# Two transformer layers on one core: the residual kept as two chunks in SBUF, larger rings, and a different order for the last 256 queries

## The chip, the core and the metric

The kernel runs on one core of a Trainium2 chip. The metric is the device time of one execution in microseconds (us). A core has five engines, each with its own in-order list of instructions: TensorE (PE in the profile, with its weight loads as PEld), VectorE (DVE), ScalarE (ACT), GpSimd (POOL), and SyncE (SP), which here issues all DMAs. The engines meet only through semaphores. SBUF is the on-chip memory of 128 partitions, PSUM holds the matrix products in eight banks of 128x512 float32 values, and HBM is the memory outside.

## The reference

Two identical layers with the same weights are applied to `x` of 2048 tokens by 512 features, in bfloat16. Each layer is a pre-norm attention with 32 heads of 16 features and a pre-norm feed-forward network (FFN) of 1792 hidden features:

```python
x = x + _A_ref(_layernorm(x), A_wqkv, A_wo)
x = x + _B_ref(_layernorm(x), B_w1, B_b1, B_w2, B_b2)
x = x + _A_ref(_layernorm(x), A_wqkv, A_wo)
x = x + _B_ref(_layernorm(x), B_w1, B_b1, B_w2, B_b2)

def _A_ref(x, wqkv, wo):
    qkv = (x @ wqkv) reshaped to q, k, v of 32 heads of 16
    p = softmax(q k^T * 16 ** -0.5)
    return (p v, heads put side by side) @ wo

def _B_ref(x, w1, b1, w2, b2):
    return gelu(x @ w1 + b1) @ w2 + b2
```

## The kernel before, in words

**Tiling.** The 2048 tokens are 16 tiles of 128 (`NT`), in four chunks of 512 queries. The residual `X` lies in SBUF whole, 16 tiles of 512 bfloat16 values per partition. Attention works in passes (`passes`, L1034). A pass takes one chunk of queries and four heads, one in each quarter of the PE rows, and goes over the key tiles. One key tile of one head for 512 queries is a *cell*: one score matmul into one PSUM bank (L1168), an exponential, and one matmul of the weights with the values, called PV (L1566). There are 4096 cells, 512 for each layer and chunk. The last chunk of the second layer is cut into two segments of 256 queries (L1044), whose cells hold two heads of 256 queries. The scores of later chunks run while the FFN of the chunk before is done in the gaps.

**Two ways to an exponential.** Most cells go to ACT, two or three at a time from one slot of PSUM banks (`exps`, L1503), into a ring of `PT_RING` = 19 units of SBUF. Units that lie in other tensors are lent to this ring for a time (`lend_units`; the profile names them kt, q and v). Cells of four key tiles of each layer (`KD`, L45) may go to DVE instead, which is 1024 of the 4096. There a cell is one instruction that turns the scores into the bits of an approximate exponential (`dfirst`, L1317), and then two that make three shifted copies of it (`dchain`, L1378 and L1380). PV takes four matmuls for such a cell, three of them with scaled copies of V (`vc`). These cells live in the buffers `DU`. `DU` = 9 means four buffers for two cells each and one for a single cell, which the profile calls dh. In the second layer there is one more for two cells, in the freed K of the first layer (kt in the profile). A cell of `KD` that finds no buffer, bank or time on DVE before its pass has run out goes to ACT as the others do (`next_act`, `next_d`, `attach`, `swap`).

**What sets the order.** The order of all instructions is written when the program is built. `_Sched.run` (L353) plays the five engines with a cost for every operation. It takes for each engine the operations whose operands are ready by that reckoning, the one with the lowest priority number first, and appends it to that engine's list with the semaphore waits that it needs. On the chip the lists are fixed. An operation that comes late there holds up all that stands behind it on its engine. Scores have priority 0. Matmuls of projections and FFN have `FPRIO` = 1.5 for the first half of a product and `MID` = 1.4 for the second, and PV has 2, or 0.5 when a ring is nearly empty. `fill` (L331) adds matmuls without use (L1156) where PE would be idle too long.

**After a segment's attention.** `norm` divides by the softmax sums and writes `OTN`. `post` (L971) then spawns `wo` (the product with Wo, added to `X` at L816), the layernorm `ln`, `hpair` (the first FFN product, seven pairs), `gelu`, and `ytile` (the second FFN product, added to `X` at L956). In the first layer follow a layernorm and the projections to K, V and Q of the second. `before(l, seg)` (L967) names the segment ahead, and three waits of the plan go by it: `ofree` in `norm`, and `xfree` and `gfree` in `post`. They keep `OTN`, `XF` and `G` from being overwritten while the segment ahead still reads them. For the second segment of 256 queries, the one ahead is the first segment of the same chunk.

**Transfers.** `loads` (L572) brings in `X` and the weights of the first projections at the start, chunks 1 to 3 of `X` with one DMA each. `wloads` (L826) brings in all later weights in pieces of 256 KB through a ring of four (`W_RING`), each when a place in the ring is free. Layernorm transposes of 128 tokens are DMAs on SP too (L637).

Of the kernel before, what the change touches and what calls it, by code (L numbers as in the profile page):

```python
# [5 lines left out]
ALU = mybir.AluOpType  # L6
ACT = mybir.ActivationFunctionType
BF16 = mybir.dt.bfloat16
# [4 lines left out]
D = 512  # L13
# [5 lines left out]
NL = 2  # L19
# [3 lines left out]
DBANK = (7,)  # L23
PT_RING = 19
LEND = (3, 2)
QP_RING = 3
W_RING = 4
W_MORE = 4
XLN_RING = 2
GP = 2  # L30

DU = 9
LNP = 7
# [18 lines left out]
EVAC = 0.4  # L52
MID = 1.4
QUEUE = 4
RUSH = 4
# [372 lines left out]
def bass_interleave_layers__mha_block__dense_activation_gelu__prompt_kernel(  # L428
# [15 lines left out]
    with ExitStack() as es:  # L444
        def sb(shape, dt, name):
            return es.enter_context(nc.sbuf_tensor(name, shape, dt))

        T = {}
        T["X"] = sb([128, NT, D], BF16, "x")
        wr = sb([128, W_RING, 1024], BF16, "wr")  # L450
# [20 lines left out]
        if DU % 2:  # L471
# [23 lines left out]
        sem_names = ["pe", "act", "dve", "pool", "dxt0", "dxt1", "dxt2", "dxt3", "dx1", "dx2", "dx3", "dwq", "dwk", "dwv", "db1", "db2"] + ["dw%d" % c for c in range(3)] + [  # L495
                     "dout"] + ["dwr%d" % i for i in range(W_RING + W_MORE)] + ["dtr%d" % i for i in range(XLN_RING)]
        sems = {n: es.enter_context(nc.semaphore("s_" + n)) for n in sem_names}
        P = _Prog(sems)
        hbm = dict(x=A_x.rearrange("b (n p) d -> p (b n) d", p=128), out=out.rearrange("b (n p) d -> p (b n) d", p=128),
                   wqkv=A_wqkv, wo=A_wo, w1=B_w1, b1=B_b1, w2=B_w2, b2=B_b2)  # L500
# [32 lines left out]
class _Plan:  # L533
# [38 lines left out]
    def loads(self):  # L572
        T, hbm = self.T, self.hbm

        def load(dst, src, sem, keys, cost):
            return _Op("sp", cost, lambda e: e.dma_start(dst, src), writes=keys, sem=sem, by=16, tail=2.0)

        def lx(c):
            return load(T["X"][:, 4 * c:4 * c + 4, :], hbm["x"][:, 4 * c:4 * c + 4, :], "dx%d" % c,
                        ["X.%d" % t for t in range(4 * c, 4 * c + 4)], 2.5)  # L580
# [22 lines left out]
        yield ("give", "loaded")  # L603

    def ln(self, tiles, dst, dkeys, prio, quick=False):

# [3 lines left out]
        for t in tiles:  # L610
            yield ("need", ("xready", t, self.phase[t // 4]))
            yield _Op("dve", 0.66, lambda e, t=t: e.bn_stats(T["STATS"][:, t, :], T["X"][:, t, :]),
                      reads=["X.%d" % t], writes=["ST.%d" % t])
            yield _Op("dve", 0.17, lambda e, t=t: e.bn_aggr(T["MV"][:, t, :], T["STATS"][:, t, :]),
                      reads=["ST.%d" % t], writes=["MV.%d" % t])
# [12 lines left out]
    def ln_tile(self, c, t, dst, dkeys, quick):  # L628
# [4 lines left out]
        yield _Op(eng, cost, lambda e: e.tensor_scalar(  # L633
            T["XLN"][:, x, :], T["X"][:, t, :], T["RSTD"][:, t:t + 1], T["NMR"][:, t:t + 1], op0=ALU.mult, op1=ALU.add),
            reads=["X.%d" % t, "RSTD.%d" % c, "NMR.%d" % c], writes=["XLN.%d" % x])
        if not quick:
# [161 lines left out]
    def wo(self, l, seg, t):  # L798
        T = self.T
        for gb in range(4):  # L800
            yield ("need", ("otn", l, seg, gb))
        us = []
        for j in range(2):
            us.append((yield ("need", ("w", l, seg, "O", j))))
        b = yield ("acq", "misc")
        pb = self.bank(b)
        q = slice((t % 4) * 128, (t % 4) * 128 + 128)
        fns = []
        for j in range(4):
# [6 lines left out]
        yield _Op("dve", DV, lambda e: e.tensor_tensor(out=T["X"][:, t, :], in0=T["X"][:, t, :], in1=pb, op=ALU.add),  # L816
                  reads=["B.%d" % b, "X.%d" % t], writes=["X.%d" % t])
        yield ("rel", "misc", b)
        yield ("give", ("xready", t, 2 * l + 1))
# [55 lines left out]
    def hpair(self, l, seg, p):  # L875
# [8 lines left out]
        for j in range(2):  # L884
# [7 lines left out]
            for h in range(0, 4, FQ):  # L892
                yield _Op("pe", FQ * MM * n / 512, fns[4 * h:4 * h + 4 * FQ],
                          reads=["WR.%d" % w] + ["XF.%d" % (t % 4) for t in self.tiles(seg)],
                          writes=["B.%d" % b], prio=MID if h else FPRIO, mode="P")
            yield from self.wdone((l, seg, "1", p), w)
# [31 lines left out]
    def ytile(self, l, seg, t):  # L928
# [9 lines left out]
        for p in range(NFC // 2):  # L938
# [15 lines left out]
            if not tail or p == last:  # L954
                yield from self.wdone(piece, w)
        yield _Op("dve", DV, lambda e: e.tensor_tensor(out=T["X"][:, t, :], in0=T["X"][:, t, :], in1=pb, op=ALU.add),  # L956
                  reads=["B.%d" % b, "X.%d" % t], writes=["X.%d" % t])
        yield ("rel", "misc", b)
        yield ("give", ("xready", t, 2 * l + 2))
        if l == NL - 1:  # L960
            yield _Op("sp", 1.0, lambda e: e.dma_start(self.hbm["out"][:, t, :], T["X"][:, t, :]), reads=["X.%d" % t],
                      writes=["OUT.%d" % t], sem="dout", by=16, tail=2.0)

    def when(self, l, seg, part):
# [57 lines left out]
    def first(self, c):  # L1022
        T = self.T
        self.phase[c] = 0
        for t in range(4 * c, 4 * c + 4):
            yield ("give", ("xready", t, 0))
        tiles = range(4 * c, 4 * c + 4)
# [633 lines left out]
```

## Time and profile before

| | |
|---|---|
| time, median of 3 runs (lowest to highest) | 1567.77 us (1567.01 to 1567.84) |
| the profiled execution's own time | 1563.99 us |
| its span, first to last instruction | 1562.1 us |
| mean granted TensorE clock | 0.992 |
| ACT busy | 1523.5 us, 98% of the span |
| PE matmuls busy | 1443.7 us, 92% |
| DVE busy | 1369.9 us, 88% |
| POOL busy | 210.5 us, 13% |
| DMA traffic, share of 16 engines | 94.14 MB, 20.8% |

Busy times come from one profiled execution; they can be set against its own time, and the median of the runs lies 3.8 us above that. A line of the profile names the source line (L1503), the engine, the operation, the tile written and the tiles read, the shapes, and how often. A wait is put down to the instruction whose semaphore came last.

### The profile page before, as it was taken

Reading aid. Unit: us, or ns where it says so; the run is one execution under the profiler, and the core shown is the slowest. Engines: PE = TensorE matmul, PEld = TensorE weight load, DVE = VectorE, ACT = ScalarE, POOL = GpSimd, SP = SyncE. Lnnn points to the kernel's source line nnn. Section 1 sums busy time; section 2 is a strip of 40 time slices with the busy share of each in tenths; the row PEclk is TensorE's granted clock in tenths of the full one; section 3 lists DMA queues with packets and bytes.
Section 4 is the critical chain, followed back from the end, with each engine's and each line's share of the span. In section 5 each row is a group of like instructions: output and inputs, shape, how many; then the busy total and the mean of one; then the engine's idle time right before and its main releaser. Section 6 shows DMA issues by size and latency. Waiting matters only on the chain.

```text
span 1562.1 us, 42238 instructions
## 1 busy us (share of the span) xinstructions
PE 1443.7 (92%) x18537; PEld 432.7 (28%) x18537; DVE 1369.9 (88%) x2653; ACT 1523.5 (98%) x1412; POOL 210.5 (13%) x250
## 2 busy tenths in 40 slices
PE   8999889999999999999989999888998989999998
PEld 2222222222222222222222222222222222233344
DVE  5689999979898989978799798999999988898893
ACT  7999999999999999999999999999999999999995
POOL 5300001002020101102030021122002010010000
PEclk9999999999999999999999899999999999999999
DMA  5100001052113310133111331001151105313430
GB/s 143 22 1 1 2 15 35 29 163 55 42 42 116 99 46 26 40 120 102 36 35 42 118 94 42 2 1 35 56 166 52 35 15 161 98 36 96 150 83 29
DMA packets 141765, 96.84 MB, mean 62 GB/s; under 512 B 36877, under 2 KB 141582, under 8 KB 141582
## 3 DMA queue, kind: packets, MB, share of 16 engines
q1 hardware_dynamic: 141582, 94.14, 20.8%
q8 instruction: 146, 2.39, 0.6%
q14 instruction: 37, 0.30, 0.1%
HBM read 84.41 MB, written 2.10 MB: 55 GB/s over the span
## 4 chain that ended last, share of the span: by engine, by line
ACT 65%; PE 24%; DVE 10%; issue 1%; DMA 0%; POOL 0%; ACTq 0%; DVEq 0%
ACT pt L1503 56%; PE ps L543 9%; PE ps L1168 8%; PE ps L1566 6%; DVE du L1317 4%; ACT g L924 3%; ACT kt L1503 2%; ACT v L1503 2%; DVE du L1380 2%; ACT q L1503 1%; DVE du L1378 1%; ACT L924 1%; DVE dh L1317 1%; ACT L1503 0%; PE ps L1156 0%
## 5 line engine op out<-in xcount | busy, mean ns | idle before, releaser
L1503 ACT ACTIVATE pt<-ps 128x1024 bf16<-128x1024 f32 (+1 forms) x1248 | 1336.7, 1232 | 10.7 <-PE ps L1168 8.0
L1168 PE MATMUL ps<-qp,kt 32*128 32x512 bf16 x4096 | 557.8, 386 | 49.7 <-ACT pt L1503 35.0
L1317 DVE TENSOR_SCALAR du<-ps 128x512 uint16<-128x512 f32 x748 | 498.9, 682 | 78.7 <-PE ps L1168 76.3
L1566 PE MATMUL ps<-pt,v 128*17 128x512 bf16 (+1 forms) x3245 | 454.2, 360 | 25.1 <-ACT pt L1503 20.2
L1566 PE MATMUL ps<-du,vc 128*17 128x512 bf16 (+1 forms) x2502 | 353.7, 360 | 8.7 <-ACT pt L1503 5.6
L1168 PEld LDWEIGHTS ps<-qp,kt 32*128 32x128 bf16 x4096 | 143.5, 91 | 611.6 <-ACT pt L1503 409.1
L1380 DVE TENSOR_SCALAR du<-du 128x2048 uint16<-128x2048 uint16 x377 | 257.6, 687 | 2.7
L1116 POOL TENSOR_SCALAR qp<-q,mask 128x512 bf16<-128x512 bf16 (+1 forms) x91 | 80.9, 889 | 958.0 <-PE ps L1168 947.8
L543 PE MATMUL ps<-xf,wr 128*32 128x512 bf16 (+1 forms) x2400 | 168.5, 368 | 1.4 <-DVE g L903 0.7
L1566 PE MATMUL ps<-du,v 128*17 128x512 bf16 (+1 forms) x834 | 160.9, 361 | 6.8 <-DVE v L770 3.1
L1378 DVE TENSOR_SCALAR du<-du 128x1024 uint16<-128x1024 uint16 x377 | 156.4, 424 | 2.5
L1566 PEld LDWEIGHTS ps<-pt,v 128*17 128x17 bf16 x3245 | 111.0, 89 | 138.3 <-issue 64.2
L543 PE MATMUL ps<-wr,g 128*32 128x512 bf16 x1600 | 126.3, 391 | 4.9 <-ACT g L924 4.3
L1566 PEld LDWEIGHTS ps<-du,vc 128*17 128x17 bf16 x2502 | 90.2, 89 | 83.3 <-issue 43.0
L1566 PE MATMUL ps<-dh,vc 128*17 128x512 bf16 (+1 forms) x330 | 95.6, 358 | 0.0
L903 DVE TENSOR_SCALAR g<-ps,hb1t 128x512 bf16<-128x512 f32 (+1 forms) x112 | 79.3, 708 | 5.4 <-PE ps L543 5.0
L1317 DVE TENSOR_SCALAR dh<-ps 128x512 uint16<-128x512 f32 x98 | 66.7, 681 | 1.2 <-PE ps L1168 1.1
L543 PEld LDWEIGHTS ps<-xf,wr 128*32 128x32 bf16 x2400 | 48.1, 95 | 63.0 <-issue 41.0
L1317 DVE TENSOR_SCALAR kt<-ps 128x512 uint16<-128x512 f32 x88 | 60.1, 683 | 5.9 <-PE ps L1168 5.0
L1156 PE MATMUL ps<-vc 128*32 128x512 bf16 x576 | 55.5, 408 | 8.3 <-DVE du L1317 7.3
L633 POOL TENSOR_SCALAR xln<-x,rstd,nmr 128x512 bf16<-128x512 bf16 x58 | 54.3, 939 | 32.9 <-DMA xf<-xln 21.2
L1566 PE MATMUL ps<-kt,vc 128*17 128x512 bf16 (+1 forms) x330 | 57.9, 338 | 0.0
(93 smaller groups left out, 1195.8 us busy)
## 6 DMA issues: line engine op xcount, KB each, us to landing
wr<-in_B_w_dram SPq DMA_DIRECT2D x256, 256.0 KB, 2.8
wr<-in_A_wqkv_dram SPq DMA_DIRECT2D x24, 256.0 KB, 2.8
wr<-in_A_wo_dram SPq DMA_DIRECT2D x18, 256.0 KB, 2.9
out_dram<-x SPq DMA_DIRECT2D x16, 128.0 KB, 2.9
g<-in_A_wqkv_dram SPq DMA_DIRECT2D x3, 512.0 KB, 6.2
x<-in_A_x_dram SPq DMA_DIRECT2D x3, 512.0 KB, 9.1
q<-in_B_w_dram SPq DMA_DIRECT2D x3, 512.0 KB, 5.0
kt<-in_B_w_dram SPq DMA_DIRECT2D x4, 256.0 KB, 3.5
```

What stands on the lines that cost most here:

```text
L543: return [lambda e, a=a: e.matmul(out[32 * a:32 * a + 32, :], lhsT=lhsT[:, 32 * a:32 * a + 32], rhs=rhs, start=start, stop=stop, tile_posi ...
L633: yield _Op(eng, cost, lambda e: e.tensor_scalar(T["XLN"][:, x, :], T["X"][:, t, :], T["RSTD"][:, t:t + 1], T["NMR"][:, t:t + 1], op0=ALU. ...
L903: yield _Op("dve", 0.21 + n / 966, lambda e, fc=fc, pb=pb: e.tensor_scalar(T["G"][:, fc, q], pb, T["HB1T"][:, fc:fc + 1], None, op0=ALU.ad ...
L924: lambda e, g=g: e.activation(out=g, in_=g, func=ACT.Gelu_apprx_tanh), reads=gk, writes=gk, prio=2)
L1116: yield _Op("pool", 0.15 + 0.62 * w / 512, lambda e, s=s, q=q, i=i, t=t, w=w: e.tensor_scalar(T["QP"][:, s, w * i:w * i + w], q, T["MASK"] ...
L1156: fns.append(lambda e, o=o, w=w, a=a, m=m: e.matmul(o, lhsT=w, rhs=rhs, start=start, stop=start, tile_position=(0, m * a)))
L1168: return (lambda e: e.matmul(o, lhsT=lhsT, rhs=rhs, start=True, stop=True, tile_position=(32 * a, 0)), ["K%d.%d.%d" % (l, gb, kt // 4), "Q ...
L1317: yield _Op("dve", 0.682, lambda e: e.tensor_scalar(u, self.bank(b), E_SCALE, E_BIAS, op0=ALU.mult, op1=ALU.add), reads=["B.%d" % b], writ ...
L1378: one = _Op("dve", 0.151 + 0.134 * n, lambda e: e.tensor_scalar(U[:, 1, 0:n, :], U[:, 0, 0:n, :], SHIFT, None, op0=ALU.add), reads=key[0], ...
L1380: two = _Op("dve", 0.152 + 0.266 * n, lambda e: e.tensor_scalar(U[:, 2:4, 0:n, :], U[:, 0:2, 0:n, :], 2 * SHIFT, None, op0=ALU.add), reads ...
L1503: yield _Op("act", 0.065 + 0.4267 * n, lambda e, src=src, dst=dst: e.activation(out=dst, in_=src, func=ACT.Exp, scale=0.25), reads=["B.%d" ...
L1566: op.fns.append(lambda e, o=o, lhsT=q[0][0][m], rhs=q[0][1][:, n * m:n * m + n], a=a, st=st, sp=sp: e.matmul(o, lhsT=lhsT, rhs=rhs, start= ...
```

## The change

It has two parts.

**The residual.** `X` has eight tiles in SBUF (`XT` = 8) instead of sixteen. Tile t lies at t modulo 8, so chunks 0 and 2 share one half and chunks 1 and 3 the other. A new tensor `kept` in HBM takes the chunk that is not in SBUF. A new thread `xfeed` for each half moves whole chunks of 512 KB through SP. Once the first layernorm of chunk h has been read, it loads chunk h + 2 from the input, and once that one's layernorm has been read, chunk h from the input again. After the first layer it stores chunk h to `kept`, loads chunk h + 2 from the input, later stores that one and loads h back, and at last, when the output of chunk h has been issued, loads h + 2 back. `wo` gets a wait of the plan for its chunk (`xin`). Chunks 2 and 3 are no longer loaded in `loads`. The 8 KB per partition that come free go to `PT_RING` (19 to 23 units of 1 KB) and to `DU` (9 to 10 cells: five buffers for two cells each, and none for a single cell).

**The last 256 queries.** `wo` and `hpair` of the last segment get priority `ENDS` = 0.9 in place of 1.5 and 1.4. `before` gives a segment ahead only if it is of another chunk, so the second segment of 256 queries no longer has the waits `ofree`, `xfree` and `gfree`. The two segments use different columns of `OTN`, `XF` and `G`.

```diff
-PT_RING = 19
+PT_RING = 23
+XT = 8
-DU = 9
+DU = 10
+ENDS = 0.9
...
-        T["X"] = sb([128, NT, D], BF16, "x")
+        T["X"] = sb([128, XT, D], BF16, "x")
...
+        kept = nc.dram_tensor("kept", [128, NT, D], BF16)
...
         for t in range(4):
-            yield load(T["X"][:, t, :], hbm["x"][:, t, :], "dxt%d" % t, ["X.%d" % t], 0.6)
+            yield load(T["X"][:, t % XT, :], hbm["x"][:, t, :], "dxt%d" % t, ["X.%d" % (t % XT)], 0.6)
+            yield ("give", ("xready", t, 0))
...
         yield lx(1)
-        yield lx(2)
-        yield lx(3)
+        for t in range(4, 8):
+            yield ("give", ("xready", t, 0))
+        yield ("spawn", self.xfeed(0), 3)
+        yield ("spawn", self.xfeed(1), 3)
...
+    def xmove(self, c, src, dst, sem, reads, writes):
+        yield _Op("sp", 1.5, lambda e: e.dma_start(dst, src), reads=reads, writes=writes, sem=sem, by=16, tail=4.0)
+
+    def xfeed(self, h):
+        keys = ["X.%d" % (t % XT) for t in range(4 * h, 4 * h + 4)]
+        x, kept = self.hbm["x"], self.hbm["kept"]
+        home = self.T["X"][:, 4 * h:4 * h + 4, :]
+        sem = "dx%d" % (h + 2)
...
+        for t in tiles(h):
+            yield ("need", ("lnt", t, 0))
+        yield from self.xmove(h, part(x, h + 2), home, sem, [], keys)
+        for t in tiles(h + 2):
+            yield ("give", ("xready", t, 0))
+        for t in tiles(h + 2):
+            yield ("need", ("lnt", t, 0))
+        yield from self.xmove(h, part(x, h), home, sem, [], keys)
+        yield ("give", ("xin", 0, h))
+        for c in (h, h + 2):
+            for t in tiles(c):
+                yield ("need", ("lnt", t, 2))
+            yield from self.xmove(h, home, part(kept, c), "dk%d" % h, keys, ["KEPT.%d" % c])
+            if c == h:
+                yield from self.xmove(h, part(x, h + 2), home, sem, [], keys)
+                yield ("give", ("xin", 0, h + 2))
+        yield from self.xmove(h, part(kept, h), home, sem, ["KEPT.%d" % h], keys)
+        yield ("give", ("xin", 1, h))
+        for t in tiles(h):
+            yield ("need", ("xout", t))
+        yield from self.xmove(h, part(kept, h + 2), home, sem, ["KEPT.%d" % (h + 2)], keys)
+        yield ("give", ("xin", 1, h + 2))
...
     def wo(self, l, seg, t):
         T = self.T
+        yield ("need", ("xin", l, seg[0]))
...
+        last = (l, seg) == (NL - 1, self.segs[l][-1])
...
-                      writes=["B.%d" % b], prio=MID if h else FPRIO, mode="P")
+                      writes=["B.%d" % b], prio=ENDS if last else MID if h else FPRIO, mode="P")
...
...
     def before(self, l, seg):
         order = [(i, x) for i in range(NL) for x in self.segs[i]]
-        return order[order.index((l, seg)) - 1] if (l, seg) != order[0] else None
+        i = order.index((l, seg)) - 1
+        return order[i] if i >= 0 and order[i][1][0] != seg[0] else None
```

The matmuls of `hpair` get the same edit of the priority as those of `wo`. Every other use of `X` is indexed by `t % XT`.

More of the change, by code (lines that the diff above doesn't have):

```diff
@@ L495, in bass_interleave_layers__mha_block__dense_activation_gelu__prompt_kernel @@
         sem_names = ["pe", "act", "dve", "pool", "dxt0", "dxt1", "dxt2", "dxt3", "dx1", "dx2", "dx3", "dwq", "dwk", "dwv", "db1", "db2"] + ["dw%d" % c for c in range(3)] + [
-                     "dout"] + ["dwr%d" % i for i in range(W_RING + W_MORE)] + ["dtr%d" % i for i in range(XLN_RING)]
+                     "dout", "dk0", "dk1"] + ["dwr%d" % i for i in range(W_RING + W_MORE)] + ["dtr%d" % i for i in range(XLN_RING)]
         sems = {n: es.enter_context(nc.semaphore("s_" + n)) for n in sem_names}
         P = _Prog(sems)
-        hbm = dict(x=A_x.rearrange("b (n p) d -> p (b n) d", p=128), out=out.rearrange("b (n p) d -> p (b n) d", p=128),
+        kept = nc.dram_tensor("kept", [128, NT, D], BF16)
+        hbm = dict(kept=kept[:, :, :], x=A_x.rearrange("b (n p) d -> p (b n) d", p=128), out=out.rearrange("b (n p) d -> p (b n) d", p=128),
                    wqkv=A_wqkv, wo=A_wo, w1=B_w1, b1=B_b1, w2=B_w2, b2=B_b2)
@@ L578, in lx @@
         def lx(c):
-            return load(T["X"][:, 4 * c:4 * c + 4, :], hbm["x"][:, 4 * c:4 * c + 4, :], "dx%d" % c,
-                        ["X.%d" % t for t in range(4 * c, 4 * c + 4)], 2.5)
+            return load(T["X"][:, 4 * c % XT:4 * c % XT + 4, :], hbm["x"][:, 4 * c:4 * c + 4, :], "dx%d" % c,
+                        ["X.%d" % (t % XT) for t in range(4 * c, 4 * c + 4)], 2.5)
         def lw(i, sem):
@@ L603, in loads, with tiles, part @@
         yield ("give", "loaded")
+    def xmove(self, c, src, dst, sem, reads, writes):
[5 more added lines that the diff above has]
+        sem = "dx%d" % (h + 2)
+        def tiles(c):
+            return range(4 * c, 4 * c + 4)
+        def part(src, c):
+            return src[:, 4 * c:4 * c + 4, :]
+        for t in tiles(h):
[20 more added lines that the diff above has]
+        yield ("give", ("xin", 1, h + 2))
     def ln(self, tiles, dst, dkeys, prio, quick=False):
@@ L611, in ln @@
             yield ("need", ("xready", t, self.phase[t // 4]))
-            yield _Op("dve", 0.66, lambda e, t=t: e.bn_stats(T["STATS"][:, t, :], T["X"][:, t, :]),
-                      reads=["X.%d" % t], writes=["ST.%d" % t])
+            yield _Op("dve", 0.66, lambda e, t=t: e.bn_stats(T["STATS"][:, t, :], T["X"][:, t % XT, :]),
+                      reads=["X.%d" % (t % XT)], writes=["ST.%d" % t])
             yield _Op("dve", 0.17, lambda e, t=t: e.bn_aggr(T["MV"][:, t, :], T["STATS"][:, t, :]),
@@ L633, in ln_tile @@
         yield _Op(eng, cost, lambda e: e.tensor_scalar(
-            T["XLN"][:, x, :], T["X"][:, t, :], T["RSTD"][:, t:t + 1], T["NMR"][:, t:t + 1], op0=ALU.mult, op1=ALU.add),
-            reads=["X.%d" % t, "RSTD.%d" % c, "NMR.%d" % c], writes=["XLN.%d" % x])
+            T["XLN"][:, x, :], T["X"][:, t % XT, :], T["RSTD"][:, t:t + 1], T["NMR"][:, t:t + 1], op0=ALU.mult, op1=ALU.add),
+            reads=["X.%d" % (t % XT), "RSTD.%d" % c, "NMR.%d" % c], writes=["XLN.%d" % x])
         if not quick:
@@ L812, in wo @@
             yield _Op("pe", FQ * MM, fns[4 * h:4 * h + 4 * FQ], reads=["WR.%d" % us[j // 2] for j in range(h, h + FQ)] + ["OTN.%d.%d" % (j, t % 4) for j in range(h, h + FQ)],
-                      writes=["B.%d" % b], prio=MID if h else FPRIO, mode="P")
+                      writes=["B.%d" % b], prio=ENDS if last else MID if h else FPRIO, mode="P")
         for j in range(2):
             yield from self.wdone((l, seg, "O", j), us[j])
-        yield _Op("dve", DV, lambda e: e.tensor_tensor(out=T["X"][:, t, :], in0=T["X"][:, t, :], in1=pb, op=ALU.add),
-                  reads=["B.%d" % b, "X.%d" % t], writes=["X.%d" % t])
+        yield _Op("dve", DV, lambda e: e.tensor_tensor(out=T["X"][:, t % XT, :], in0=T["X"][:, t % XT, :], in1=pb, op=ALU.add),
+                  reads=["B.%d" % b, "X.%d" % (t % XT)], writes=["X.%d" % (t % XT)])
         yield ("rel", "misc", b)
@@ L894, in hpair @@
                           reads=["WR.%d" % w] + ["XF.%d" % (t % 4) for t in self.tiles(seg)],
-                          writes=["B.%d" % b], prio=MID if h else FPRIO, mode="P")
+                          writes=["B.%d" % b], prio=ENDS if last else MID if h else FPRIO, mode="P")
             yield from self.wdone((l, seg, "1", p), w)
@@ L955, in ytile @@
                 yield from self.wdone(piece, w)
-        yield _Op("dve", DV, lambda e: e.tensor_tensor(out=T["X"][:, t, :], in0=T["X"][:, t, :], in1=pb, op=ALU.add),
-                  reads=["B.%d" % b, "X.%d" % t], writes=["X.%d" % t])
+        yield _Op("dve", DV, lambda e: e.tensor_tensor(out=T["X"][:, t % XT, :], in0=T["X"][:, t % XT, :], in1=pb, op=ALU.add),
+                  reads=["B.%d" % b, "X.%d" % (t % XT)], writes=["X.%d" % (t % XT)])
         yield ("rel", "misc", b)
@@ L960, in ytile @@
         if l == NL - 1:
-            yield _Op("sp", 1.0, lambda e: e.dma_start(self.hbm["out"][:, t, :], T["X"][:, t, :]), reads=["X.%d" % t],
+            yield _Op("sp", 1.0, lambda e: e.dma_start(self.hbm["out"][:, t, :], T["X"][:, t % XT, :]), reads=["X.%d" % (t % XT)],
                       writes=["OUT.%d" % t], sem="dout", by=16, tail=2.0)
+            yield ("give", ("xout", t))
     def when(self, l, seg, part):
@@ L1024, in first @@
         self.phase[c] = 0
-        for t in range(4 * c, 4 * c + 4):
-            yield ("give", ("xready", t, 0))
         tiles = range(4 * c, 4 * c + 4)
```

## The prediction

> **What bounds the kernel now.** I read the engine totals first. Their line gives, per engine, the busy time, its share of the span and the instructions.
>
> ```profile
> span 1562.1 us, 42238 instructions
> ...
> PE 1443.7 (92%) x18537; PEld 432.7 (28%) x18537; DVE 1369.9 (88%) x2653; ACT 1523.5 (98%) x1412; POOL 210.5 (13%) x250
> ```
>
> ACT leaves only 1562.1 - 1523.5 = 38.6 us. The waits of ACT alone say where those are (who <- for whom: total us, times, longest):
>
> ```profile
> ACT pt L1503 <- PE ps L1168: 8.0, 12, 2.1
> ACT xf L650 <- PE ps L644: 7.7, 1, 7.7
> ACT kt L650 <- PE ps L644: 4.8, 1, 4.8
> ACT g L898 <- PE ps L543: 3.5, 2, 2.6
> ACT pt L1503 <- PE ps L1566: 2.0, 2, 1.7
> ```
>
> Between the first and last exponential ACT loses about 11 us (8.0 + 2.0 + 1.0 on its v units). The rest is the start and the end. Time therefore falls in three ways only: less work for ACT, fewer of those 11 us, a shorter end.
>
> Less work for ACT means more cells on DVE. ACT had 3162 cells (two-wide calls: 842 + 25 + 17 + 13; three-wide: 406 + 21 + 20 + 9) and DVE 934 of its 1024. Cut at every 512th cell, in order of time, the line of DVE's first step (L1317) gives (stretch: length, DVE busy and count, clock, DMA share, GB/s):
>
> ```profile
> 0.00:206.00 206.00, 65.55 (x98) 1.00 0.12 32
> 206.00:395.00 189.00, 81.15 (x124) 0.99 0.21 61
> 395.00:587.00 192.00, 75.68 (x114) 1.00 0.24 70
> 587.00:779.00 192.00, 75.67 (x114) 0.99 0.23 66
> 779.00:968.00 189.00, 79.89 (x121) 0.96 0.23 67
> 968.00:1156.00 188.00, 81.87 (x125) 1.00 0.15 42
> 1156.00:1341.00 185.00, 84.31 (x129) 0.99 0.28 83
> 1341.00:1532.00 191.00, 76.25 (x114) 1.00 0.28 82
> ```
>
> The reader is to see that a stretch with 114 DVE cells takes 192 us and one with 129 takes 185: 7/15 = 0.47 us for each cell that ACT is spared. The groups agree. All exponentials take ACT about 1441 us (1523.5 less 82 for GELU, copies and table loads), which is 0.456 us a cell, and a three-wide call is 1515 - 1096 = 419 ns longer than a two-wide one. I take 0.45.
>
> The end I read from the chain of waits and the PE timeline after the last exponential (1533.3 us). Columns: start, us, what.
>
> ```profile
> 1536.46 1.48 PE L543 MATMUL ps<-q,g 128*32 128x512 bf16 x24 [0.98 <-ACT g L924]
> 1537.75 0.62 PE L543 MATMUL ps<-wr,otn 128*32 128x512 bf16 x8
> ...
> 1540.13 0.62 PE L543 MATMUL ps<-wr,otn 128*32 128x512 bf16 x8
> 1540.56 2.78 PE L543 MATMUL ps<-q,g 128*32 128x512 bf16 x48
> ...
> 1545.17 0.72 PE L644 MATMUL ps<-ident,xln 128*128 128x128 bf16 x8 [1.19 <-DVE xln L633]
> ...
> 1546.50 3.68 PE L543 MATMUL ps<-xf,kt 128*32 128x256 bf16 x128 [0.28 <-DVE xf L652]
> ```
>
> The second halves of Wo for the last two tiles (`wr,otn`) stand among the second FFN product of the segment before (`q,g`), and the layernorm behind them leaves PE idle.
>
> **Part 1, the larger rings.** *DU from 9 to 10 cells.* The first layer had 9 cells of buffer, the second 11. The ordinary stretches of the first layer average (124 + 114 + 114)/3 = 117 cells and those of the second (121 + 125 + 129)/3 = 125. The one added cell is half of that step: +4 in each of three stretches, 12. The first stretch starts late for another reason (its shifted V copies are made until 48.6 us, its DVE is 99% busy from 120 to 200 us) and the last runs out of cells, so +2 each. The second layer's middle is near the limit of 128: 0. Sum 16 cells x 0.45 = 7.2 us. Part of the 8 us step may come from the projections that only the first layer has; then it is less. Ends: nothing, or all 90 remaining cells (40 us). Downwards: a new written order could bring the three good stretches to the 114 of the others, 7 + 11 + 15 = 33 cells, +15 us.
>
> *No single-cell buffer.* 98 cells ran as singles: 285 + 418 ns of copies against (419 + 684)/2 = 552 in a pair. DVE saves 98 x 0.15 = 15 us. DVE isn't the bound, so this costs and gives nothing directly; it pays for 16 x (682 + 552 ns) = 20 us of new DVE work, within DVE's 192 idle us.
>
> *PT_RING from 19 to 23.* ACT waited for PV, which frees the ring, 3.0 us in all (2.0, and 1.0 on v). At most 3 us, I take 0. [...]
>
> **Part 2, the residual through HBM.** Seven moves of 512 KB for each half, 14 in place of two: 12 more. Their issue is on SP, which waits most of the time for free weight places (553.3 + 540.4 us of waits of L860), and their 6.3 MB add 7% to 94.14 MB that fill 20.8% of the DMA engines. What matters is lateness. The planner reckons 1.5 + 4.0 us for a move. The trace has two rows of that size:
>
> ```profile
> x<-in_A_x_dram SPq DMA_DIRECT2D x3, 512.0 KB, 9.1
> q<-in_B_w_dram SPq DMA_DIRECT2D x3, 512.0 KB, 5.0
> ```
>
> The 9.1 us are three transfers behind three others; 5.0 is nearest to a lone one, so a move is as reckoned (ends -0.5 and +3.6 us each). Layernorm stats and Wo take their data later than that by far: chunk h + 2 is asked for by Wo a whole stretch (190 us) after its move could start, and at the start the normalized tiles of chunks 2 and 3 are written by POOL at 33 to 53 us only, since transposes are spread. The start hides the moves: 0. Chunk 3 can be asked for once chunk 1's tiles are written at 27 us and is there by 36 even at 9.1. Four moves wait for the store just ahead of them on the same half, and two for output stores; while SP waits, weight loads stand behind. The four-place weight ring is their cover; if a weight is late, PE stops in its list, and scores with it. I cost it at 0, with an upper end in the rivals. [...]
>
> **Part 3, the end.** With priority 0.9 the second halves of Wo come as soon as the last heads are normalized (1536.67): at about 1536.9 and 1537.3 in place of 1537.75 and 1540.13. The residual add of the second tile ends at about 1538.8 instead of 1541.66, and all that follows on its chain (stats, POOL's power, transposes, copies: 1541.56 to 1546.35, 4.8 us) moves up with it. PE has work meanwhile: the other segment's two tiles, 6.4 us, and Wo, 0.9, from 1536.46 fill it to 1543.8; then transposes. Hidden FFN starts near 1544.1 instead of 1546.50: -2.4 us. From there PE is the bound (12.79 us for its 344 matmuls) as before. The check is PE's idle time, 1.19 + 0.5 + 0.3 and some filler, about 2.3 us, which is also the limit. The dropped waits: `xfree` and `gfree` were met at 1544.72, before the transposed tiles at 1546.35, so they didn't bind in the old order but would bind the new by 0.6 us; `ofree` could hold PV at about 1440 us, where ACT is 39.7 of 40 us busy: 0. Late next: PE's own 20 us of work after the last exponential.
>
> **Sum.** -7.2 - 2.4 = -9.6 us, on the profiled execution 1563.99 to 1554.4. The median before is 3.8 us above that execution, so I put it on the median: 1567.8 - 9.6 = 1558.2.
>
> **The rivals.** *No more cells on DVE.* Cells may be limited by PSUM banks and by the rule that a pass near its end gives its cells to ACT, not by buffers. For it: DVE is 88% busy and still left cells. Against: 117 against 125. Then 1567.8 - 2.4 = 1565.4.
>
> *Slower: late moves stop PE.* A move that takes 9.1 us holds SP 3.6 us beyond the reckoning, and ACT has one other score slot of about 1.1 us as cover: 2.5 us lost each. With all six waiting moves uncovered that is +15, net 1573; it ends the gain at four and makes the kernel slower by 0.2% only at all six. Against it: the four-place ring, and that few moves meet a busy weight stream.
>
> *The new order loses clock.* Near 218 us and 877 us ACT stops for 2.9 and 2.6 us while the granted clock is 0.72 and 0.80 over those stretches. Six such more, in an order written anew, cost 16 us: 1575.
>
> *Far more cells.* If buffers were the limit everywhere and half of the 90 cells move: 20 + 2.4 us, 1545.
>
> **How the numbers follow.** 0.2%, 3 us, is about what a measurement tells from no change. Forecast, with its own range 1552 to 1564: 0.58. No more cells: 0.16, of which 0.04 falls beyond 3 us on either side. Late moves 0.10, lost clock 0.08, far more cells 0.08. Faster: 0.58 + 0.08 + 0.02 = 0.68; same 0.12; slower 0.10 + 0.08 + 0.02 = 0.20. The range takes in the forecast, the first rival and half of the others: 1546 to 1574.
>
> **What would show it.** About 950 instructions on the line of DVE's first step, all in pairs, and some 16 fewer cells on ACT, with ACT busy near 1516; stretches of the first layer near 189 us; 14 moves of 512 KB landing in 5 to 6 us, with no PE wait on DMA; hidden FFN of the last segment 10.8 us after the last exponential instead of 13.2. Wrong it would be if ACT's waits grow beyond 11 us, if the count on DVE stays at 934, or if DVE's new work delays evacuations that scores wait for.

## The result, and the profile after

| | before | changed |
|---|---|---|
| median (lowest to highest), executions | 1567.80 us (1567.01 to 1569.34), 4 | 1556.26 us (1554.76 to 1557.44), 4 |
| ratio, 95% interval | | 0.9917 [0.9899, 0.9934] |
| the profiled execution's own time, span | 1563.99, 1562.1 us | 1557.44, 1555.7 us |
| its mean granted clock | 0.992 | 0.995 |
| last exponential ends at, span behind it | 1533.3, 28.8 us | 1529.3, 26.3 us |
| cells on DVE | 934 | 938 |

The change makes the kernel 0.8% faster. The forecast was 1558.2, so the time came out 2 us below it, well within its range. The sum was right, by luck; the reason for most of it was not, as the rest shows. First a discrepancy: the medians differ by 11.5 us and the profiled executions by 6.6 only. The profiled execution of before lies 3.8 us under its median, that of after 1.2 us above. Something outside the fixed order of the program moves an execution by several microseconds.

The page of the changed kernel begins:

```profile
span 1555.7 us, 42439 instructions
...
PE 1440.4 (93%) x18678; PEld 431.6 (28%) x18678; DVE 1371.4 (88%) x2571; ACT 1521.7 (98%) x1407; POOL 203.7 (13%) x250
```

ACT's work fell by 1523.5 - 1521.7 = 1.8 us only, and DVE's busy time is the same to 1.5 us. The waits of ACT in the changed kernel (who <- for whom: total us, times, longest):

```profile
ACT pt L1549 <- PE ps L1214: 7.0, 14, 1.0
ACT kt L694 <- PE ps L688: 4.9, 1, 4.9
ACT xf L694 <- PE ps L688: 4.0, 1, 4.0
ACT pt L1549 <- PE ps L1612: 1.5, 3, 1.0
ACT g L944 <- PE ps L546: 1.3, 2, 1.1
```

Waits on scores (L1214) went from 8.0 to 7.0, waits on PV for a free unit of the ring (L1612) from 3.0, in two groups, to 1.5. The wait for the last layernorm (xf) went from 7.7 to 4.0. DVE's first step of a cell by stretches of 512 cells (length, DVE busy and count, clock, DMA share, GB/s):

```profile
0.00:204.00 204.00, 65.53 (x100) 1.00 0.15 38
204.00:394.00 190.00, 80.10 (x121) 1.00 0.23 67
394.00:582.00 188.00, 81.07 (x123) 0.98 0.26 71
582.00:776.00 194.00, 74.01 (x110) 0.99 0.25 75
776.00:966.00 190.00, 78.76 (x118) 0.99 0.25 73
966.00:1156.00 190.00, 78.53 (x118) 0.99 0.15 42
1156.00:1341.00 185.00, 84.70 (x128) 1.00 0.28 83
1341.00:1529.00 188.00, 80.44 (x121) 1.00 0.31 87
```

The third stretch gained 9 cells, the last 7 and the first 2; the second, fourth, fifth, sixth and seventh lost 3, 4, 3, 7 and 1. On these lines that is nothing in all: a cell that runs across a cut is counted on both sides of it, five times before and once here. Counted once each, the cells rose from 934 to 938. The end of PE's list:

```profile
1531.95 1.05 PE L546 MATMUL ps<-wr,otn 128*32 128x512 bf16 x16 [1.33 <-DVE otn L834]
1532.81 2.78 PE L546 MATMUL ps<-q,g 128*32 128x512 bf16 x48
...
1537.46 0.68 PE L688 MATMUL ps<-ident,xln 128*128 128x128 bf16 x8
1538.07 1.05 PE L546 MATMUL ps<-q,g 128*32 128x512 bf16 x16
1538.95 3.23 PE L546 MATMUL ps<-xf,kt 128*32 128x256 bf16 x112
```

Both second halves of Wo now come in one piece ahead of the other segment's FFN, and no idle time is left between the second of them and the last segment's first FFN product (`xf,kt`). That product starts 9.6 us after the last exponential in place of 13.2. Part of the other segment's FFN now stands behind it, so the end is shorter by 2.5 us and not by 3.6. The moves of the residual, with KB each and us to landing:

```profile
x<-in_A_x_dram SPq DMA_DIRECT2D x7, 512.0 KB, 4.3
kept<-x SPq DMA_DIRECT2D x4, 512.0 KB, 2.9
x<-kept SPq DMA_DIRECT2D x4, 512.0 KB, 3.9
```

They are quicker than the planner's 5.5 us. The waits of SP show what stands behind them:

```profile
SPq L906 <- PE ps L1214: 805.3, 159, 168.1
...
SPq L612 <- DMA kept<-x: 9.2, 4, 2.3
...
SPq L612 <- DMA out_dram<-x: 4.9, 2, 2.7
```

SP waits 14 us for stores in the whole execution, against 805 us for free places of the weight ring in one group alone. On the path stand only PE's waits for weights behind such places, 2.1 us after against 1.0 before, and DVE's 1.0 us for the first load of X at the start (1.2 before).

### The profile page after: what moved, and what is told of

It reads as the page before. It is cut to its first block, busy times and chain, and to the rows that moved or that the text cites. A ratio compares the mean times of both kernels' runs of the same rounds, so it can differ in the third digit from the quotient of the medians.

```text
span 1555.7 us, 42439 instructions
## 1 busy us (share of the span) xinstructions
PE 1440.4 (93%) x18678; PEld 431.6 (28%) x18678; DVE 1371.4 (88%) x2571; ACT 1521.7 (98%) x1407; POOL 203.7 (13%) x250
## 4 chain that ended last, share of the span: by engine, by line
ACT 61%; PE 26%; DVE 13%; issue 1%; DMA 0%; ACTq 0%
ACT pt L1549 53%; PE ps L546 9%; PE ps L1214 8%; PE ps L1612 8%; DVE du L1363 5%; ACT g L970 3%; DVE du L1426 2%; ACT v L1549 2%; DVE du L1424 1%; ACT kt L1549 1%; ACT q L1549 1%; DVE kt L1363 1%; ACT L1549 1%; ACT L970 1%; DVE x L862 0%
## 5 line engine op out<-in xcount | busy, mean ns | idle before, releaser
L1549 ACT ACTIVATE pt<-ps 128x1024 bf16<-128x1024 f32 (+1 forms) x1285 | 1376.0, 1233 | 9.5 <-PE ps L1214 7.0
L1363 DVE TENSOR_SCALAR du<-ps 128x512 uint16<-128x512 f32 x859 | 571.2, 681 | 84.8 <-PE ps L1214 82.4
L1214 PE MATMUL ps<-qp,kt 32*128 32x512 bf16 x4096 | 552.8, 386 | 53.1 <-ACT pt L1549 41.0
L1612 PE MATMUL ps<-pt,v 128*17 128x512 bf16 (+1 forms) x3362 | 440.8, 360 | 19.7 <-ACT pt L1549 16.1
L1612 PE MATMUL ps<-du,vc 128*17 128x512 bf16 (+1 forms) x2892 | 374.4, 359 | 10.0 <-ACT pt L1549 5.5
L1214 PEld LDWEIGHTS ps<-qp,kt 32*128 32x128 bf16 x4096 | 141.9, 91 | 609.1 <-ACT pt L1549 432.6
L1426 DVE TENSOR_SCALAR du<-du 128x2048 uint16<-128x2048 uint16 (+1 forms) x435 | 297.0, 687 | 3.3
L1162 POOL TENSOR_SCALAR qp<-q,mask 128x512 bf16<-128x512 bf16 (+1 forms) x91 | 70.1, 770 | 966.9 <-PE ps L1214 956.8
L1424 DVE TENSOR_SCALAR du<-du 128x1024 uint16<-128x1024 uint16 (+1 forms) x435 | 179.4, 426 | 3.1
L1612 PE MATMUL ps<-du,v 128*17 128x512 bf16 (+1 forms) x964 | 169.9, 361 | 11.8 <-ACT pt L1549 7.5
L1612 PEld LDWEIGHTS ps<-pt,v 128*17 128x17 bf16 x3362 | 106.8, 88 | 132.2 <-issue 67.8
L1612 PEld LDWEIGHTS ps<-du,vc 128*17 128x17 bf16 x2892 | 96.0, 89 | 97.1 <-issue 48.0
L829 POOL TENSOR_TENSOR ott<-xt,rc 128x256 bf16<-128x256 f32 x42 | 32.2, 766 | 208.9 <-DVE rc L821 180.3
L1612 PEld LDWEIGHTS ps<-du,v 128*17 128x17 bf16 x964 | 43.3, 88 | 56.0 <-issue 16.5
L1612 PE MATMUL ps<-kt,vc 128*17 128x512 bf16 (+1 forms) x303 | 49.3, 334 | 0.4 <-DVE kt L1426 0.4
```

The costliest lines, as they stand in the source:

```text
L1162: yield _Op("pool", 0.15 + 0.62 * w / 512, lambda e, s=s, q=q, i=i, t=t, w=w: e.tensor_scalar(T["QP"][:, s, w * i:w * i + w], q, T["MASK"] ...
L1214: return (lambda e: e.matmul(o, lhsT=lhsT, rhs=rhs, start=True, stop=True, tile_position=(32 * a, 0)), ["K%d.%d.%d" % (l, gb, kt // 4), "Q ...
L1363: yield _Op("dve", 0.682, lambda e: e.tensor_scalar(u, self.bank(b), E_SCALE, E_BIAS, op0=ALU.mult, op1=ALU.add), reads=["B.%d" % b], writ ...
L1424: one = _Op("dve", 0.151 + 0.134 * n, lambda e: e.tensor_scalar(U[:, 1, 0:n, :], U[:, 0, 0:n, :], SHIFT, None, op0=ALU.add), reads=key[0], ...
L1426: two = _Op("dve", 0.152 + 0.266 * n, lambda e: e.tensor_scalar(U[:, 2:4, 0:n, :], U[:, 0:2, 0:n, :], 2 * SHIFT, None, op0=ALU.add), reads ...
L1549: yield _Op("act", 0.065 + 0.4267 * n, lambda e, src=src, dst=dst: e.activation(out=dst, in_=src, func=ACT.Exp, scale=0.25), reads=["B.%d" ...
```

## The experiments

Each group of runs had executions of the kernel before beside it: 1569.18 us (27 executions) for the first four runs, 1567.80 (19) for the next four, 1569.12 (13) for the last. Cells and matmuls without use are counted in the program. In the table, "clock" is the mean over the executions of a program, "at 0.995" is the mean time moved to that clock at 1.0 us for each 0.001 (the lines of time against clock within single programs run from 0.8 to 1.3, so a shift by 0.007 is good to 1 or 2 us), and "idle" is the share of all positions of a 3.4 us window, in the profiled execution, in which PE is busy less than 60% (3.41 us is the shortest half-clock stretch in the traces).

| program | median us | ratio to before, 95% | clock | at 0.995 | cells | idle |
|---|---|---|---|---|---|---|
| before, three groups | 1569.2, 1567.8, 1569.1 | | 0.9879, 0.9897, 0.9881 | 1562.4, 1562.6, 1562.3 | 934 | 1.8% |
| changed | 1556.3 | 0.9917 [0.9899, 0.9934] | 0.9962 | 1557.4 | 938 | 1.0% |
| before, once more | 1567.9 | 0.9989 [0.9975, 1.0004] | 0.9893 | 1562.7 | 934 | 1.7% |
| end alone | 1564.1 | 0.9964 [0.9949, 0.9980] | 0.9885 | 1558.1 | 937 | 1.8% |
| residual alone, rings 19, 9 | 1569.5 | 0.9996 [0.9980, 1.0012] | 0.9941 | 1568.5 | 925 | 1.2% |
| changed without the end | 1559.5 | 0.9924 [0.9906, 0.9941] | 0.9967 | 1560.5 | 934 | 1.2% |
| before, more filling | 1564.4 | 0.9981 [0.9969, 0.9993] | 0.9934 | 1563.0 | 934 | 1.4% |
| changed, more filling | 1554.2 | 0.9914 [0.9894, 0.9934] | 0.9988 | 1558.2 | 938 | 0.7% |
| before, order of DV 0.70 | 1565.2 | 0.9982 [0.9962, 1.0002] | 0.9917 | 1562.1 | 930 | 1.3% |
| changed, order of DV 0.70 | 1553.6 | 0.9905 [0.9879, 0.9931] | 0.9928 | 1550.8 | 947 | 1.2% |
| before, order of DV 0.67 | 1580.6 | 1.0078 [1.0057, 1.0100] | 0.9940 | 1580.3 | 911 | 1.5% |
| changed, order of DV 0.72 | 1561.1 | 0.9953 [0.9936, 0.9970] | 0.9900 | 1554.9 | 945 | 1.0% |
| residual alone, rings 20, 9 | 1569.0 | 1.0005 [0.9991, 1.0018] | 0.9941 | 1568.9 | 933 | 1.4% |
| changed, DV 0.68, more filling | 1551.9 | 0.9892 [0.9877, 0.9907] | 0.9983 | 1555.4 | 955 | 0.8% |

### The kernel before, once more

No edit.

> The kernel before, unedited, to see the granted clock of every execution. The profiled executions differ by 6.5 us (1563.99 and 1557.44), the medians by 11.5. Theory A (clock): the other executions of the kernel before lost more TensorE clock than the profiled one (0.992); then executions near 1568 show a clock near 0.988 and time falls by about 1 us for each 0.001 of clock. Theory B (nothing but the work on ACT): the executions scatter by 2 to 4 us with no relation to the clock.

Theory A holds. Over the 27 executions of before beside it the clock ran from 0.985 to 0.992, and time falls along a line of 1.2 us for each 0.001 (correlation -0.94); in the other programs the line lies between 0.8 and 1.3. The three groups of before, at clocks of 0.9879 to 0.9897, come out at 1562.3 to 1562.6 when moved to 0.995. The executions profiled show where the time goes. This execution had a clock of 0.985 and a span of 1571.8 us:

```profile
ACT pt L1503 <- PE ps L1168: 14.5, 24, 1.9
```

The same program in the same order, at 0.992, has 8.0 us on this line. And the windows of the kernel before, around the GELU at 865 us, show what precedes a loss of clock (stretch: length, then busy us of PE, PEld, DVE, ACT, POOL with counts, granted clock, DMA):

```profile
858.00:864.80 6.80, 6.80 (x96) 2.01 (x92) 5.90 (x12) 6.77 (x7) 0.69 (x1) 1.00 0.14 42
864.80:868.20 3.40, 1.22 (x17) 0.34 (x13) 3.33 (x7) 3.40 (x2) 0.00 (x0) 1.00 0.01 3
868.20:878.50 10.30, 9.52 (x74) 2.23 (x66) 4.28 (x8) 7.83 (x5) 0.00 (x0) 0.50 0.42 128
878.50:885.00 6.50, 6.50 (x93) 1.92 (x94) 5.59 (x9) 6.36 (x6) 0.00 (x0) 1.00 0.35 105
```

In the second stretch ACT does GELU, and PE's list stops at a matmul of the second FFN product that reads the GELU's output:

```profile
868.00 0.88 PE L543 MATMUL ps<-wr,g 128*32 128x512 bf16 x8 [1.88 <-ACT g L924]
```

PE is busy 1.22 of 3.40 us there, and the next 10.3 us run at half clock, in which ACT loses 2.5 us. Apart from the last microseconds of a program, there are 57 half-clock stretches in the 14 profiled executions. All begin behind 3.4 us in which PE was busy less than 80%, 37 of them behind less than 60%, and last a multiple of 3.41 us. In the profiled execution of before the granted clock was 0.50 for 3.41 us at 216.3, 683.9, 922.8 and 1274.4 us and for 10.24 us at 868.2 us; in that of the changed kernel for 6.83 us at 512.1 us and for 3.41 us at 686.2, 798.9 and 1010.5 us. PE was not always near idle ahead of them: in before it was busy 52% of the 3.41 us ahead of the stretch at 683.9 us, and 69% ahead of the one at 922.8 us.

Within one execution all half-clock stretches start on one grid of 3.413 us (to 3 ns; in before the starts at 216.27 and 1274.40 us lie 310 such steps apart), and the grid begins at another phase in each execution: 1.23 us after the span's start in one profiled execution of before, 2.33 us in the other, 0.14 us in that of the changed kernel. How busy PE was in a full-rate window of this grid goes with the chance that the next window runs at half rate, but does not settle it (start and end of the programs left out):

| PE busy in the window | windows | followed by half rate |
|---|---|---|
| under 40% | 5 | 5 |
| 40 to 60% | 73 | 33 |
| 60 to 70% | 151 | 17 |
| 70 to 80% | 518 | 2 |
| 80% and more | 5522 | 0 |

The changed kernel keeps PE busier during the same GELU, and here the clock is whole:

```profile
862.00:868.80 6.80, 6.59 (x84) 1.85 (x76) 6.73 (x12) 6.58 (x7) 0.69 (x1) 1.00 0.17 56
868.80:872.20 3.40, 2.31 (x26) 0.69 (x25) 3.40 (x8) 3.39 (x3) 0.00 (x0) 1.00 0.14 47
872.20:882.40 10.20, 9.38 (x129) 3.03 (x125) 8.74 (x16) 10.17 (x9) 0.00 (x0) 1.00 0.48 156
```

This is one execution. On its grid the windows during the GELU were busy 83% and 79%; with another phase one could have fallen on these 2.31 of 3.40 us, and by the table windows of 60 to 70% do lose the clock at times (17 of 151). GELU is not the only such place either. The five windows under 40% lie under GELU and its table load, but for 37 of the 57 stretches ACT did neither in the window ahead.

### The end alone

```diff
+ENDS = 0.9
...
-        return order[order.index((l, seg)) - 1] if (l, seg) != order[0] else None
+        i = order.index((l, seg)) - 1
+        return order[i] if i >= 0 and order[i][1][0] != seg[0] else None
```

and the priority `ENDS` for `wo` and `hpair` of the last segment, on the kernel before.

> The kernel before with the edits for the last 256 queries alone (priority 0.9, no waits between the two halves), X whole in SBUF, rings 19 and 9. DVE has 937 cells in this program, 934 in the one before. Theory A (each edit has its own price): 2.4 us for the end and 3 x 0.45 us for cells, so -3.8 us, near 1564. Theory B (the gain came from the new order as a whole and its clock): -2.4 us or less for the end, the rest unforeseeable, within 3 us of 1566.

The ratio 0.9964 means -5.6 us (1.8 us more than theory A's, with an interval of 3.1 to 8.0). The clock is nearly that of before, 0.9885 against 0.9879, so about 0.6 us of it is clock. The span behind the last exponential is 26.8 us, 2.0 less than before; three cells are 1.4 us. Theory A's -3.8 lies within the interval. The time, 1564.1, lies within 3 us of 1566 too, so it does not rule out theory B; that the clock stayed speaks against it. On the changed kernel the same edits do much less to the end itself, as its counterpart shows below.

### Residual alone

On the changed kernel:

```diff
-PT_RING = 23
+PT_RING = 19
-DU = 10
+DU = 9
-ENDS = 0.9
...
-        return order[i] if i >= 0 and order[i][1][0] != seg[0] else None
+        return order[order.index((l, seg)) - 1] if (l, seg) != order[0] else None
```

with the old priorities in `wo` and `hpair`. The order written for this program changes part of the computation: the output of the second chunk of 512 queries is not the reference's. All instructions and transfers are there, so the time is that of the same work. The run with rings of 20 and 9 below does not have this fault and takes the same time.

> X as two chunks and the 14 moves, but rings of 19 and 9 as before and no edit of the end; the 8 KB per partition are left unused. DVE has 925 cells in this program. Theory A (cells): 9 cells more on ACT, +4 us, near 1572, and the moves themselves cost nothing. Theory B (moves stop PE): more than +7 us, with PE or DVE waiting on DMA or on weights. Theory C (moves help, since fewer loads crowd the start): not above 1568.

None of the three as it stands. In time it equals before (0.9996), but at a clock of 0.9941 in place of 0.9879. At equal clock it is 6 us slower: 4.1 us more work on ACT for 9 cells, and for the rest the lists show only small waits. Theory B finds little support in the lists of waits: POOL waits 27 us for transposes (23 before), PE 2.3 us for weights (1.0 before), ACT for no DMA.

### The change without the end

```diff
-ENDS = 0.9
...
-        return order[i] if i >= 0 and order[i][1][0] != seg[0] else None
+        return order[order.index((l, seg)) - 1] if (l, seg) != order[0] else None
```

> The changed kernel without the edits of the end: X as two chunks, rings of 23 and 10. DVE has 934 cells, as before the change. Theory A (cells and end add up): against the changed kernel 2.4 us for the end and 4 x 0.45 us for cells are lost, near 1560.5, and against the kernel before 7 us are gained that no cell explains. Theory B (the rings do nothing by themselves): near 1566 to 1568.

1559.5 with a ratio of 0.9924 is theory A's number. So most of the gain, 0.0076 of 0.0083 by the ratios, comes with the residual and the rings, though the program has not one cell more on DVE than before (934). What it has is clock: 0.9967, and that is worth about 9 us against 0.9879. The span behind its last exponential is 26.6 us already. The new order puts the second halves of Wo ahead of the other segment's FFN with the old priorities too, so that in this kernel the edits of the end bring 0.3 us there and the four cells.

### More filling, before and after

```diff
-WARM = 0.38
+WARM = 0.45
```

> The kernel before with one constant changed: WARM, the share of PE activity below which the planner adds matmuls without use, is 0.45 in place of 0.38. The program has 970 such matmuls in place of 662, and the order of all other work is the same, with 934 cells on DVE. Theory A (the gain of the change is granted clock, lost after stretches in which PE does little): the mean clock rises from 0.988 toward 0.995 and the time falls by 1.1 to 1.2 us for each 0.001, so by 6 to 8 us, near 1562. Theory B (the clock is a companion of the gain and not its cause): time within 2 us of the kernel before, 1569, or above it, since the added matmuls stand ahead of scores.

Theory A in direction and half of its size. Everything but the added 308 matmuls stands in the same order as before, the clock rises from 0.9897 to 0.9934, and the time falls by 3.0 us on a ratio of 0.9981 (interval 1.1 to 4.9). At equal clock the times are the same to 0.4 us (1562.6 and 1563.0). Added work in an unchanged order can't shorten the time by itself, so the clock is a cause of time and no companion. Its profiled execution, at 0.997, shows the score wait that the executions of before show with 8.0 and 14.5:

```profile
ACT pt L1503 <- PE ps L1168: 5.9, 10, 1.5
```

During the GELU at 865 us its two emptiest windows of the grid have PE busy 58% and 64%, where before had one of 36%, and the clock stays whole.

> The changed kernel with the same one constant (0.45): 1050 matmuls without use in place of 770, 938 cells on DVE as before. Theory A: the clock rises from 0.996 to 0.998 or more, so at most 4 us are to be had, near 1553. Theory B: no change, 1556, or slower.

0.9988 and 1554.2: 2.0 us less than the changed kernel, though each comes from another group of runs and the intervals of the two ratios overlap.

### The same work in another order

```diff
-DV = 0.69
+DV = 0.70
```

on both kernels. `DV` is the planner's cost of some operations of DVE. The edit changes no operation, only what the planner reckons.

> The kernel before with one cost of the planner changed by 0.01 us (DV from 0.69 to 0.70), which is no change of any work but writes another order: 930 cells on DVE (934 before), 770 matmuls without use (662 before). Theory A (which stretches PE spends idle is an accident of the order): the clock moves by several thousandths from 0.988, up since there are more such matmuls, and the time with it, 1561 to 1568. Theory B (the change itself, by its rings or its moves, is what keeps PE busy): clock 0.988 and time 1569 plus 2 us for 4 cells.

Clock 0.9917 against 0.9897 beside it: up, by two thousandths. Time 0.9982 of before, with an interval that reaches no change. It speaks for theory A, weakly.

> The changed kernel with the same 0.01 us in the planner's cost: 947 cells on DVE (938), 646 matmuls without use (770). Theory A (accident of the order): the clock falls below 0.996, to near 0.990, which costs 7 us, and 9 cells bring 4: near 1559. Theory B (the change keeps PE busy in any order): clock 0.996, time 1552.

The clock fell, as theory A says, but to 0.9928 only, which costs 3 us against the changed kernel. The time is nearer to theory B's 1552 than to theory A's 1559: at equal clock this order is 6.6 us faster, more than its 9 cells at 0.45. ACT's work is 4.9 us less (1516.8); where the other 1.7 us come from is open. An edit of 0.01 us in one constant moves the two things that this change was to be judged by, 9 cells and three thousandths of clock.

That made me count the cells over orders, in programs that were not all run: both kernels with DV from 0.65 to 0.73 in steps of 0.01, and X in two chunks with rings of 20 and 9.

```
DV                      0.65 0.66 0.67 0.68 0.69 0.70 0.71 0.72 0.73   mean
before                   918  923  911  933  934  930  931  919  926    925
X in two chunks, 20, 9   935  931  930  933  933  933  932  930  931    932
changed, 23, 10          933  936  937  955  938  947  944  945  945    942
```

Over orders the change brings 17 cells. Of these, 10 come with the step from rings of 20 and 9 to 23 and 10 together with the edits of the end, which by themselves brought 3 in the kernel before; the other 7 come with the residual in two chunks and one unit of the ring. The kernel before was the best of its nine orders, the changed one stands fourth lowest of its nine. Matmuls without use show no such shift (means of 741 before, 730 changed), while the two kernels compared have 662 and 770: near the lower end of one list and the highest of the other.

### Two more orders

DV 0.67 on the kernel before, DV 0.72 on the changed one.

> The kernel before in one more order (the planner's cost DV 0.67 in place of 0.69): 911 cells on DVE (934 before), 806 matmuls without use (662). Theory A (time = cells at 0.45 us each, plus 1.0 to 1.2 us for each 0.001 of clock): at an equal clock 10 us above the kernel before. Its clock, if the clock is an accident of the order, may be anywhere from 0.986 to 0.995, so 1570 to 1580. Theory B (a cell on DVE spares ACT little, other waits take its place): within 4 us of the kernel before at an equal clock.

1580.6, just above theory A's range, and at equal clock 18 us above before instead of 10. ACT's work grew by 10.1 us for 23 cells, 0.44 each, as reckoned:

```profile
PE 1443.6 (92%) x18606; PEld 433.8 (28%) x18606; DVE 1349.5 (86%) x2606; ACT 1533.6 (97%) x1410; POOL 202.2 (13%) x250
```

Over all 14 profiled executions ACT's busy time falls along a line of 0.46 us for each cell on DVE (correlation -0.99). Most of the rest is a wait that the order added:

```profile
ACT pt L1503 <- PE ps L1566: 8.2, 4, 6.4
```

ACT waits on PV for units of the ring of 19, on this line 6.2 us more than before.

> The changed kernel in one more order (DV 0.72): 945 cells on DVE (938), 758 matmuls without use (770). Theory A: 3 us below the changed kernel at an equal clock, so 1553 at 0.996; the clock, as an accident of the order, anywhere from 0.988 to 0.997. Theory B (X in two chunks keeps PE busy whatever the order): clock 0.994 or more, as in the three programs with X in two chunks whose order was not moved by DV.

The clock is 0.9900, so theory B falls: X in two chunks does not keep the clock by itself. At equal clock the program is 2.5 us under the changed kernel for 7 cells, as theory A has it. At its own clock it is at 0.9953 of before, little more than half of the gain of the changed kernel.

### Residual alone, with rings of 20 and 9

The edit is that of the residual alone, with `PT_RING = 20`.

> X as two chunks and the 14 moves, rings of 20 and 9, no edit of the end: 933 cells on DVE, one fewer than the kernel before, 774 matmuls without use. Theory A (the moves cost nothing, the rest is cells and clock): at an equal clock within 2 us of the kernel before; in time, lower by 1.0 to 1.2 us for each 0.001 of clock above it, so near 1562 to 1564 if the clock is 0.994 as it was with rings of 19 and 9. Theory B (the moves cost by themselves what the run with rings of 19 and 9 cost beyond its 9 cells, some 3 us): 3 us above that.

Neither. At 0.9941 it takes as long as before (1.0005), 6.6 us more at equal clock. The work on ACT is 1.9 us more; the waits name most of the rest:

```profile
ACT pt L1548 <- PE ps L1611: 5.2, 2, 4.1
...
ACT kt L1548 <- PE ps L1611: 2.5, 2, 2.1
```

These 7.7 us, and 0.4 more on units in v, are waits on PV for ring units, against 3.0 before. In five of the six programs with a ring of 23 these waits come to between 1.0 and 1.8 us, and to 3.3 in the sixth. With the smaller rings it depends on the order: 1.8, 3.0, 3.5, 8.1, 9.0. No engine on the path waits for a move; PE waits 1.8 us for weights.

### The two together

```diff
-DV = 0.69
+DV = 0.68
-WARM = 0.38
+WARM = 0.45
```

> The changed kernel with DV 0.68 and WARM 0.45: 955 cells on DVE (938), 1026 matmuls without use. Theory A: 17 cells x 0.45 = 7.6 us below the changed kernel, and a clock of 0.998 gives 2 us more: 1546 to 1549, below every kernel so far. Theory B (cells and clock do not add up, since the added matmuls stand ahead of scores): not below 1552.

1551.85 us, 0.9892 of before. It beats both kernels, misses theory A's 1549 and lies at theory B's line of 1552. ACT's work is 7.1 us under that of the changed kernel, as 17 cells promise, and the clock was 0.9983; but at equal clock only 2.0 us are gained (1557.4 to 1555.4). Waits on PV took 1.8 us of the difference (1.5 to 3.3); the rest is not accounted for.

```profile
PE 1448.5 (94%) x18988; PEld 435.6 (28%) x18988; DVE 1381.7 (89%) x2600; ACT 1514.6 (98%) x1411; POOL 207.0 (13%) x250
```

## Why the prediction was right, and where not

**What bounds it.** Right. ACT is busy 97% to 98% of the span in all 14 profiled executions, and a cell on DVE spares ACT 0.44 to 0.46 us, where 0.45 was used.

**DU from 9 to 10, "+16 cells, 7.2 us".** This step failed for the two kernels compared: +4 cells, 1.8 us. A count that stays at 934 was named as a sign of being wrong, and 938 is next to it. It took the buffers for the only thing that decides the count. Over nine orders the means are nearer to it (+17 for the whole change, +10 for the step of the rings and the end), but DU alone was never varied, and one order differs from the next by as much: from 911 to 934 before, from 933 to 955 after. A rise of that size was read from stretches that differ by more than that among themselves.

**No single-cell buffer, "DVE saves 98 x 0.15 = 15 us".** That it gives nothing to the time directly fits. The saving was put too high: it was worked out from the mean durations of records that overlap. In the changed kernel DVE's records sum to 1537.7 us where it is busy for 1371.4. The change without the end has the same 934 cells as before and no single buffer, and DVE's busy time is 2.2 us less (1367.7 for 1369.9).

**PT_RING, "at most 3 us, I take 0".** On the two kernels waits on PV fell by 1.5 us (3.0 before, 1.5 after). Its worth seems larger where the order is less lucky: with rings of 19 and 20 these waits were 9.0 and 8.1 us in two orders, with a ring of 23 at most 3.3 in six programs.

**The residual through HBM, "0".** Right for the moves. They land in 2.9 to 4.3 us, in place of the 5.5 reckoned, and nobody on the path waits for them. The stores to HBM landed in 2.9 us, sooner than the loads of the same size (3.9 and 4.3). X in two chunks was 6 to 7 us slower at equal clock with the old rings, in two programs. What the lists show of that are cells and waits on PV, that is, a worse order in those two; over nine orders X in two chunks has more cells in the mean (932 against 925), so this is no fixed price.

**The end, "-2.4 us".** Right in size: 28.8 us behind the last exponential became 26.3. That the edits of the end are its cause holds for the kernel before, where they alone bring 2.0 us. Without them the order written for the larger rings already has 26.6, while X in two chunks with the old rings has 28.8; so in the changed kernel they add 0.3 us. PE is the bound in that stretch as foreseen: in the changed kernel it is busy for all of the 13.05 us from 1538.95 us to 1552.00.

**The clock, a rival that pointed the wrong way.** "The new order loses clock" was priced at 16 us to the slow side. It won about 0.008 of clock instead, from 0.988 to 0.996, worth 8 us at 1.0 us for each 0.001, or 6 to 10 by the lines of the groups of before. With 2.4 us for the end, 1.8 for cells and 1.5 for waits on PV that is 14 us, against 11.5 to 12.9 measured (1567.8 and 1569.2 for before). The prediction's sum had 0 for the largest of these terms and 7.2 for one that measured 1.8. That the two errors nearly cancelled is luck. The profiled execution of before had lost seven windows of clock, another of the same program fourteen, and I read the price of a lost window from the trace without asking how many there usually are.

**What stays open.** Whether the two chunks and the larger rings favour the clock at all. The orders with X whole had 0.988 to 0.9897 (before), 0.9885, 0.9917 and 0.9940; those with X in two chunks 0.9962, 0.9967, 0.9941, 0.9941, 0.9928 and 0.9900. The means, 0.991 and 0.994, lean that way, but the ranges overlap, and more orders would be needed to tell. The number of matmuls without use does not settle it either: the kernel before in the order of DV 0.70 has 770 of them, as many as the changed kernel, and a clock of 0.9917. That the change does not bring the clock gain in every order is shown by the run with DV 0.72, which has all of the change and a clock of 0.9900.

## What to carry to other kernels

Where an order is written by a planner, an edit rewrites all of it; reorder both versions by a change that does no work, such as 0.01 us in one cost, and see how far the counts and the clock move, before a gain is put down to the edit. Compare executions at equal granted clock, and look for the stretches just ahead of each half-clock window: the emptiest of them were GELU blocks of 9 us, and matmuls without use where PE had little to do were worth 3 us. A buffer's worth may show in the waits of unlucky orders, and not in those of the one at hand.

## What the runs showed of the hardware

Within one program time follows the granted clock closely, 0.8 to 1.3 us for each 0.001 with correlations of -0.86 to -0.99, though PE is not the busiest engine (93% of the span in the changed kernel, ACT 98%). The clock was lost in steps of 3.41 us at a granted clock of 0.50, and PE was still at work ahead of them: it was busy 0.15 to 0.75 of the 3.4 us before over the 57 stretches, 0.33 to 0.69 in the two kernels compared. The same program lost seven such windows in one execution and fourteen in another; the grid of windows had another phase in each (1.23 and 2.33 us after the span's start), so the windows fell differently on the same stretches. Stores of 512 KB from SBUF to HBM landed in 2.9 us, sooner than loads of that size (3.9 and 4.3).
